# A two-layer token mixer on one core: another load list, layer-1 grouping and TensorE order

## The chip, the core and the metric

The kernel runs on one NeuronCore of a Trainium2 chip. Its engines run side by side, each with its own instruction stream: TensorE (PE in the profile; its weight loads are PEld) multiplies matrices, VectorE (DVE), ScalarE (ACT) and GpSimd (POOL) work on elements, and SyncE (SP) issues most of the DMAs. Streams are ordered among each other only by semaphores. Operands live in SBUF, 128 partitions wide; matmul results go to PSUM, from where ACT and DVE take them. The metric is the device time of one execution in microseconds (us), lower is better.

## What is computed

The input x has 2048 tokens of 512 features in bf16; w1 and w2 are 512×512, w3 is 512×1792 and w4 is 1792×512.

```
h  = gelu(layernorm(x) @ w1)
hs = [quarter 0 of h moved by +1 token, quarter 1 by -1, quarter 2 by +2, quarter 3 by -2] @ w2
x1 = x + hs
out = x1 + gelu(layernorm(x1) @ w3) @ w4
```

Tokens shifted in from outside are zeros. The layer norms have no learned weights.

## The kernel before

**Tiles.** The 2048 tokens are 16 tiles of 128. A tile's layer norm is numbered q: 0 to 15 are the first layer norm, 16 to 31 the second (q = 16 + tile). Everything of x, the weights, the hidden layers and the normalised tiles stays in SBUF.

**One token tile's way.** Its x is loaded (L368). Statistics come either from DVE (bn_stats L416, bn_aggr L418) or, for the q in `STAT_ACT`, from ACT passes that sum (L395, L400) and small DVE steps (L405, L408, L412). POOL raises the variance to the power -0.5 (L423). The normalisation runs on DVE (L445), ACT (L454) or POOL (L457), as `NORM` says for that q; for ACT and POOL a further small step, nmr (L450), runs on DVE or POOL as `NMR` says. The normalised tile is then transposed, either by TensorE into PSUM (L490; `ty:q` in the order) with a copy back by ACT, DVE or half each (`EVAC`, L498), or by a transposing DMA that SP issues (`tp`, L463). Tiles that have a `ty` or `sa` in the order go by TensorE, and a `tp` entry for them in the load list is then skipped.

**Matmuls.** `up1:g` (L626) multiplies a group of tiles by w1; `GROUPS[1]` lists how many tiles each group holds, in tile order. A gelu on ACT (L641) moves the result to hT. `mix:t` (L666) multiplies the shifted h of one tile by w2, so it needs h of the tile and of its two neighbours; DVE adds x and writes x1 (L673, L677), after which the second layer norm of the tile starts. `up2:g` multiplies a group of tiles by w3 in 14 chunks of 128 features, up to 1024 columns of PSUM at a time, each followed by a gelu on ACT. `down:t` (L695) multiplies one tile by w4 in 14 matmuls, DVE adds x1 (L703), and the tile is stored (L706). The last tile goes in three parts of 256, 160 and 96 columns (`TAIL`).

**Tile 0** goes another way, to start early. It is centred only, its x is the stationary operand: `sa:0 sb:0` are the two halves of its transposition, `ra:0 rb:0` the two halves of its product with w1 (L528; part a reads the first half of w1, part b the second), a gelu on ACT with the scale (L569) follows, then `th:0` transposes the result on TensorE (L594) and DVE copies it (L604, `HEV`).

**Warm-up.** `warm:n` is n matmuls on zeros (L720) before the first real work.

**Who orders what.** The order on TensorE is `SCRIPT` (L274), written out. `LOADS` (L271) is the order of the loads: `x4-5` is one DMA of two tiles, `@act` puts a load on ACT's ring instead of SP's, `w1a` and `w1b` are halves of a weight, a bare `w3` is all of it. The loads' priority puts them ahead of everything else on SP. The streams of ACT, DVE, POOL and SP are made by a planner (`order` and `place`): it computes from TensorE's order when each operation is due, starting at `DUE`, adds the wishes of `BIAS`, and plays the program through with written-down durations, taking on each engine the most urgent operation that is ready within a look-ahead (`LOOK`). `LAG` is what it adds to a load's landing. The planner runs on the host, and only the order of the instructions comes from it. On the chip each engine runs its stream strictly in that order.

In PSUM there are three pairs of banks for y (transposed tiles, up1, up2) and two single banks for o (warm-up, th, mix, down), each used in turn.

Of the kernel before, what the change touches and what calls it, by code (L numbers as in the profile page):

```python
# [25 lines left out]
class Program:  # L26
# [2 lines left out]

    HOP = {"pe": 200.0, "dve": 155.0, "act": 220.0, "pool": 120.0, "sp": 70.0}  # L30
    LOOK = {"dve": 300.0, "act": 300.0}
    DUE = 164483.0
    BEGIN = {"sp": 30.0, "act": 150.0, "pe": 400.0, "dve": 150.0, "pool": 450.0}
    ENTRY = 1900.0
    COLD, RESTART = 4300.0, 800.0
    LAG = {"load": 750, "tp": 700}

    def __init__(self):
        self.ops = []
# [12 lines left out]
    def order(self):  # L52
# [58 lines left out]
        assert seen == len(self.ops), "cycle"  # L111
        if self.DUE:

            topo, left = [], [len(d) for d in preds]
            stack = [i for i, n in enumerate(left) if n == 0]
            while stack:
                i = stack.pop()
                topo.append(i)
                for j in succs[i]:
                    left[j] -= 1  # L120
                    if left[j] == 0:
                        stack.append(j)
            due, t = {}, self.DUE
            for op in self.ops:
# [12 lines left out]
        for op in self.ops:  # L137
            op.prio += BIAS.get(op.name, 0.0)
            if op.first is not None:
# [11 lines left out]
    def place(self, succs, order_only):  # L151
# [46 lines left out]
        def land(op):  # L198
            nonlocal moved, last
            if op.queue == "tp":  # L200
                at = max(clock + 500.0, op.start + 2450.0, last + 600.0) + self.LAG["tp"]
            elif op.name.startswith("out"):
                at = clock + 300.0
                self.total = max(self.total, at)
            else:
                moved += op.dur
                at = clock + 600.0 + min(600.0, 0.3 * moved) + (600.0 if op.dur > 1400.0 else 0.0)
                at += self.LAG["load"] if moved > 1200.0 else 50.0
            if op.queue != "tp":
# [47 lines left out]
        self.seq = out  # L257
        return out

GROUPS = {1: (1, 1, 1, 1, 2, 1, 4, 2, 2, 1), 2: (2, 4, 4, 2, 4)}  # L260
NORM = {0: "act", 3: "act", 7: "pool", 8: "act", 9: "pool", 10: "pool", 11: "pool", 12: "pool", 14: "act", 15: "act", 16: "pool", 18: "act", 19: "act", 24: "pool", 25: "act", 26: "pool", 27: "pool", 29: "pool", 30: "pool", 31: "act"}
EVAC = {0: "both", 1: "both", 2: "both", 4: "both", 8: "both", 9: "dve", 10: "dve", 11: "dve", 12: "dve", 13: "dve", 14: "dve", 16: "dve", 17: "dve", 19: "both", 20: "both", 21: "both", 22: "both", 23: "both", 24: "dve", 25: "both", 27: "both", 29: "both", 30: "both", 31: "both"}
STAT_ACT = (0, 7, 9, 12, 13, 15, 18, 21, 25, 29, 30)
TAIL = (256, 160, 96)
NMR = {0: "pool", 1: "pool", 3: "pool", 5: "pool", 6: "pool", 7: "pool", 8: "pool", 9: "pool", 11: "pool", 13: "pool", 14: "pool", 15: "pool", 16: "pool", 17: "pool", 18: "pool", 20: "pool", 21: "pool", 22: "pool", 26: "pool", 27: "pool", 28: "pool", 29: "pool", 31: "pool"}
NAT = (0,)
SPLIT = (0,)
CSPLIT = ()
HEV = {0: "dve", 4: "dve"}
BIAS = {}  # L270
LOADS = """  # L271
x1 x2 tp2 x0@act w1a w1b x3 x4-5 tp5 w2a w2b x6-7 w3 tp17 w4a x8-10 w4b tp6 x11-12 tp1 tp16 x13-15
"""
SCRIPT = """  # L274
warm:9 sa:0 sb:0 ty:1 ra:0 rb:0 ty:2 up1:1 th:0 up1:2 mix:0 ty:3 ty:5 mix:1 ty:4 up1:3-4 ty:16 mix:2 ty:17
mix:3 up2:0 mix:4 up1:5 down:1 down:0 mix:5 up1:6-7 mix:8 mix:6 up1:9 mix:9-10 up1:8 mix:7 mix:11 up2:1
mix:13 mix:15 up2:3 down:5 mix:12 up2:2 mix:14 down:2 down:4 down:3 down:6-8 down:11 down:9 up2:4 down:10
down:12-15
"""

def bass_standalone__mixer_s_mlp__prompt_kernel(nc, x, w1, w2, w3, w4, out):
# [3 lines left out]
    NT, DC, FC = S // P, D // P, F // P  # L285
    groups = {l: [(sum(GROUPS[l][:i]), n) for i, n in enumerate(GROUPS[l])] for l in GROUPS}
    NXN, NO, NPAIR, NOB, NJ = 16, 4, 3, 2, 4
# [8 lines left out]
    with ExitStack() as es:  # L296
# [87 lines left out]
        def ln(layer, t):  # L384
# [3 lines left out]
            col = lambda a: a[:, q : q + 1]  # L388
            how = NORM.get(q, "dve")
            sign = -1.0 if q in NAT and how == "act" else 1.0  # L390
            if q in STAT_ACT:
                if layer == 1:
# [22 lines left out]
            else:  # L415
# [4 lines left out]
                       writes=[(("mv", q), 0), (("vpe", q), 0)], dur=75)  # L420
            var = vpe[:, q : q + 1] if q in STAT_ACT else mv[:, q, 1:2]
            pg.add("pool", f"rstd{q}",
# [3 lines left out]
            if q in NAT:  # L426
                assert how != "act" or q in STAT_ACT

# [18 lines left out]
            else:  # L447
                eng = NMR.get(q, "dve")
                pg.add(eng, f"nmr{q}",
# [17 lines left out]
        def pe_transpose(t, q, pair):  # L467
            layer = 1 if q < NT else 2
            how = EVAC.get(q, "act")
            if pair:  # L470
# [104 lines left out]
        def h_transpose(t):  # L575
            g = group_of[1, t]
            how = HEV.get(t, "act")
            k = NAT.index(t)
# [71 lines left out]
        def mm_mix(t):  # L650
# [20 lines left out]
            wr = [(("x1", t), 0)]  # L671
            if NT + t in STAT_ACT:
                f = lambda e: e.scalar_tensor_tensor(x1_sb[:, t, :], dst, 1.0, x_sb[:, t, :], ALU.mult, ALU.add,  # L673
# [198 lines left out]
```

## Time and profile before

| what | value |
|---|---|
| median of 4 runs | 135.41 us (135.33 to 135.69) |
| the profiled execution's own time | 135.33 us |
| its span, first to last instruction | 134.0 us |
| granted TensorE clock | 1.0 all through |
| POOL, busiest 40th of the span | 0.9 of the slice |
| HBM read, written | 6.82 MB, 2.10 MB |

When the loads went out and landed, in us from the start of the span:

| load | issued | landed after |
|---|---|---|
| x1, x2 (SP) | 0.08, 0.54 | 2.4, 2.6 |
| x0 (ACT) | 0.21 | 2.6 |
| w1a, w1b | 0.99, 1.46 | 4.3, 4.5 |
| x3, x4-5 | 2.07, 2.5 | 4.3, 4.6 |
| w3 (1792 KB) | 4.51 | 9.3 |
| x8-10 | 5.57 (SP held 3.5) | 13.2 |
| w4b | 9.15 (SP held 1.9) | 12.1 |

SP's first transposing DMA (tile 6) was issued at 15.33, then x11-12 and x13-15, then six more transposes from 19.21 on. The second up1 group that needs a transposing DMA started at 30.8.

How to read it: a busy share is an average over the whole span, so it doesn't tell which engine sets the end. The chain of waits does: it goes back from the last instruction, at each step to what released it. A TensorE piece in the chain that follows another TensorE piece without a gap means that TensorE was never waiting there.

### The profile page before, as it was taken

How to read it: one execution, taken by the hardware profiler on the slowest of the kernel's cores; microseconds unless marked ns; L12 is line 12 of the kernel's file. 1: busy time of each engine (PE TensorE's matmuls, PEld its weight loads, DVE VectorE, ACT ScalarE, POOL GpSimd, SP SyncE). 2: the span in 40 equal slices, each digit the busy share in tenths (PEclk: the TensorE clock that was granted, in tenths of full speed). 3: DMA queues.
4: the chain of work that ended last, by engine and by line, in shares of the span. 5: the costliest groups of instructions: out<-in, count | busy, mean ns of one | idle time of the engine just before them, and what ended most of it. 6: DMA issues, size and time to landing. Idle time of an engine off the chain costs nothing.

```text
span 134.0 us, 2001 instructions
## 1 busy us (share of the span) xinstructions
PE 130.9 (98%) x776; PEld 71.7 (53%) x789; DVE 50.2 (37%) x134; ACT 58.4 (44%) x92; POOL 29.8 (22%) x68
## 2 busy tenths in 40 slices
PE   8999999999999999999999999999999999999994
PEld 3487687544666444478444444444444444444464
DVE  2799976756188920070070004232222200012223
ACT  6798359979625375547225553000000155520000
POOL 2444449892103850015010002100000000000000
PEclk9999999999999999999999999999999999999999
DMA  5999998555452134100311000311111100001112
GB/s 156 306 387 395 352 282 235 89 81 110 86 116 84 39 77 82 39 0 18 65 39 39 0 0 0 78 39 44 39 41 66 49 0 0 0 5 39 39 39 78
DMA packets 21290, 12.19 MB, mean 91 GB/s; under 512 B 13857, under 2 KB 20769, under 8 KB 21281
## 3 DMA queue, kind: packets, MB, share of 16 engines
q1 hardware_dynamic: 20704, 11.80, 33.2%
q10 hardware_dynamic: 576, 0.26, 0.7%
q8 instruction: 6, 0.10, 0.3%
q14 instruction: 4, 0.02, 0.1%
HBM read 6.82 MB, written 2.10 MB: 67 GB/s over the span
## 4 chain that ended last, share of the span: by engine, by line
PE 94%; DMA 3%; SPq 1%; issue 1%; DVE 0%
PE y_ps L626 46%; PE o_ps L695 36%; PE o_ps L666 10%; DMA w_sb<-in_w_dram 3%; PE y_ps L490 1%; SPq L368 1%; PE y_ps L528 0%; SPq L377 0%; DVE o_sb L703 0%; PE o_ps L594 0%; SPq L857 0%
## 5 line engine op out<-in xcount | busy, mean ns | idle before, releaser
L626 PE MATMUL y_ps<-xnT,w_sb 128*128 128x512 bf16 (+2 forms) x421 | 63.4, 308 | 0.2
L626 PEld LDWEIGHTS y_ps<-xnT,w_sb 128*128 128x128 bf16 x424 | 38.3, 98 | 24.9
L641 ACT ACTIVATE h2T<-y_ps 128x1024 bf16<-128x1024 f32 (+1 forms) x29 | 28.6, 994 | 48.8 <-PE y_ps L626 48.6
L695 PE MATMUL o_ps<-w_sb,h2T 128*128 128x512 bf16 (+3 forms) x247 | 48.6, 355 | 0.3
L695 PEld LDWEIGHTS o_ps<-w_sb,h2T 128*128 128x128 bf16 x252 | 23.6, 98 | 24.7
L703 DVE TENSOR_TENSOR o_sb<-o_ps,x_sb 128x512 bf16<-128x512 f32 (+3 forms) x18 | 11.4, 631 | 46.9 <-PE o_ps L695 46.9
L423 POOL TENSOR_TENSOR rstd<-mv,neghalf 128x1 f32<-128x1 f32 x21 | 11.5, 549 | 22.9 <-DVE mv L418 14.0
L416 DVE BATCH_NORM_STATS2 st<-x_sb 128x6 f32<-128x512 bf16 x21 | 14.1, 678 | 3.3 <-DMA x_sb<-in_x_dram 3.2
L666 PE MATMUL o_ps<-w_sb,hT 128*128 128x512 bf16 x59 | 14.9, 379 | 0.3
L423 POOL TENSOR_TENSOR rstd<-vpe,neghalf 128x1 f32<-128x1 f32 x11 | 6.0, 548 | 29.4 <-DVE vpe L412 29.3
L673 DVE SCALAR_TENSOR_TENSOR x_sb<-o_ps,x_sb 128x512 bf16<-128x512 f32 x5 | 3.4, 683 | 19.0 <-PE o_ps L666 19.0
L641 ACT ACTIVATE hT<-y_ps 128x512 bf16<-128x512 f32 (+1 forms) x10 | 8.1, 805 | 5.1 <-PE y_ps L626 5.0
L666 PEld LDWEIGHTS o_ps<-w_sb,hT 128*128 128x128 bf16 x64 | 6.0, 98 | 5.7
L677 DVE TENSOR_TENSOR x_sb<-o_ps,x_sb 128x512 bf16<-128x512 f32 x11 | 7.5, 683 | 3.7 <-PE o_ps L666 3.6
L457 POOL TENSOR_SCALAR xn_buf<-x_sb,rstd,nmr 128x512 bf16<-128x512 bf16 x11 | 8.4, 765 | 0.8 <-DVE nmr L450 0.4
L400 ACT ACTIVATE junk<-x_sb 128x512 bf16<-128x512 bf16 x11 | 6.9, 624 | 2.2 <-DVE x_sb L673 2.2
L454 ACT ACTIVATE xn_buf<-x_sb,nmr,rstd 128x512 bf16<-128x512 bf16 x8 | 6.3, 807 | 1.2 <-POOL nmr L450 1.1
L445 DVE TENSOR_SCALAR xn_buf<-x_sb,mv,rstd 128x512 bf16<-128x512 bf16 x12 | 5.3, 443 | 2.8 <-POOL rstd L423 2.6
L720 PE MATMUL o_ps<-zeros 128*128 128x512 bf16 x9 | 4.0, 631 | 0.4 <-DVE zeros L347 0.4
L395 ACT ACTIVATE junk<-x_sb 128x512 bf16<-128x512 bf16 x6 | 3.7, 624 | 0.7 <-DMA x_sb<-in_x_dram 0.7
L418 DVE BATCH_NORM_AGGREGATE mv<-st 128x2 f32<-128x9 f32 x21 | 3.8, 189 | 0.3
L450 POOL TENSOR_SCALAR nmr<-mv,rstd 128x1 f32<-128x1 f32 x13 | 3.4, 263 | 0.7
(34 smaller groups left out, 28.5 us busy)
## 6 DMA issues: line engine op xcount, KB each, us to landing
out_dram<-o_sb SPq DMA_DIRECT2D x15, 128.0 KB, 1.7
w_sb<-in_w_dram SPq DMA_DIRECT2D x1, 1792.0 KB, 9.3
w_sb<-in_w_dram SPq DMA_DIRECT2D x2, 896.0 KB, 11.8
w_sb<-in_w_dram SPq DMA_DIRECT2D x4, 256.0 KB, 4.7
x_sb<-in_x_dram SPq DMA_DIRECT2D x3, 256.0 KB, 5.1
x_sb<-in_x_dram SPq DMA_DIRECT2D x2, 384.0 KB, 9.5
x_sb<-in_x_dram SPq DMA_DIRECT2D x3, 128.0 KB, 2.6
xnT<-xn_buf SPq DMA_TRANSPOSE x24, 2.5
```

The costliest lines, as they stand in the source:

```text
L400: (lambda d: (lambda e: e.activation(d, src, ACT_F.Square, accum_out=sums[:, q, 1:2])))(junk[:, b, :]),
L416: pg.add("dve", f"bnst{q}", lambda e: e.bn_stats(st9[:, q, 0:6], src), reads=rs, writes=[(("st", q), 0)], dur=605)
L423: lambda e: e.tensor_tensor(col(rstd), var, neghalf[:], ALU.pow),
L445: lambda e: e.tensor_scalar(dst, src, mv[:, q, 0:1], rstd[:, q : q + 1], ALU.subtract, ALU.mult),
L454: f = lambda e: e.activation(dst, src, ACT_F.Identity, bias=nmr[:, q : q + 1], scale=rstd[:, q : q + 1])
L457: f = lambda e: e.tensor_scalar(dst, src, rstd[:, q : q + 1], nmr[:, q : q + 1], ALU.mult, ALU.add)
L626: ins = e.matmul(y_ps[:, p, W * i : W * (i + 1)], wsb[:, dc, P * fc : P * (fc + 1)], src[:, dc, P * t0 : P * t0 + W], start=(dc == 0), sto ...
L641: (lambda d, s: (lambda e: e.activation(d, s, ACT_F.Gelu_apprx_tanh)))(dst, ysrc),
L666: ins = e.matmul(dst, hT[:, j, c0 : c0 + P], w2_sb[:, j, :], start=(j == 0), stop=(j == DC - 1))
L677: f = lambda e: e.tensor_tensor(x1_sb[:, t, :], dst, x_sb[:, t, :], ALU.add)
L695: ins = e.matmul(dst, h2T[:, fc, P * t : P * (t + 1)], w4_sb[:, fc, cs], start=(fc == 0), stop=(fc == FC - 1))
L703: (lambda d, c: (lambda e: e.tensor_tensor(o_sb[:, oi, c], d, x1_sb[:, t, c], ALU.add)))(dst, cs),
```

## The change

The load list is rewritten: x0 and x1 come in one load on SP's ring, first of all; x3, x4 and x5 come alone; w3 comes in two halves with x6 between; w4 is one load, after x7-9 and x11; x10, x15 and x12-14 follow it. The `tp` entries all name tiles that TensorE transposes.

Layer 1's groups change from tiles 0, 1, 2, 3, 4-5, 6, 7-10, 11-12, 13-14, 15 to 0, 1, 2, 3, 4, 5, 6-7, 8-9, 10-13, 14-15. The order on TensorE changes: eleven warm-up matmuls instead of nine; `mix:0` and `mix:1` together after `ty:3`; `up1:5` ahead of `up2:0`; other sequences of mix, up2 and down later. The tables that place statistics, normalisation and copies on engines change, `BIAS` is filled, and two constants of the planner change.

```
-    DUE = 164483.0
+    DUE = 30468.4
...
-    LAG = {"load": 750, "tp": 700}
+    LAG = {"load": 450, "tp": 700}
...
-GROUPS = {1: (1, 1, 1, 1, 2, 1, 4, 2, 2, 1), 2: (2, 4, 4, 2, 4)}
+GROUPS = {1: (1, 1, 1, 1, 1, 1, 2, 2, 4, 2), 2: (2, 4, 4, 2, 4)}
-NORM = {0: "act", 3: "act", 7: "pool", 8: "act", 9: "pool", 10: "pool", 11: "pool", 12: "pool", 14: "act", 15: "act", 16: "pool", 18: "act", 19: "act", 24: "pool", 25: "act", 26: "pool", 27: "pool", 29: "pool", 30: "pool", 31: "act"}
+NORM = {0: "act", 4: "act", 5: "act", 6: "pool", 8: "pool", 9: "pool", 10: "act", 11: "act", 12: "act", 13: "pool", 14: "act", 15: "act", 18: "pool", 19: "pool", 20: "pool", 21: "act", 24: "act", 28: "act", 29: "act", 30: "pool", 31: "act"}
-EVAC = {0: "both", 1: "both", 2: "both", 4: "both", 8: "both", ... }
+EVAC = {0: "dve", 2: "both", 4: "both", 5: "dve", 8: "dve", ... }
-STAT_ACT = (0, 7, 9, 12, 13, 15, 18, 21, 25, 29, 30)
+STAT_ACT = (0, 9, 12, 14, 15, 20, 23, 24, 25, 27, 30)
...
-HEV = {0: "dve", 4: "dve"}
-BIAS = {}
+HEV = {0: "dve", 4: "dve", 5: "dve", 6: "dve"}
+BIAS = {"bnag15": 607.808, "bnag16": -502.345, "bnag2": -211.967, ... "nmr7": 1640.92, ... "x1_8": -1394}
 LOADS = """
-x1 x2 tp2 x0@act w1a w1b x3 x4-5 tp5 w2a w2b x6-7 w3 tp17 w4a x8-10 w4b tp6 x11-12 tp1 tp16 x13-15
+tp4 x0-1 x2 w1a w1b tp17 x3 x4 x5 w2a w2b tp5 tp3 tp5 w3a x6 w3b x7-9 x11 tp1 w4 tp0 x10 x15 x12-14
 """
 SCRIPT = """
-warm:9 sa:0 sb:0 ty:1 ra:0 rb:0 ty:2 up1:1 th:0 up1:2 mix:0 ty:3 ty:5 mix:1 ty:4 up1:3-4 ty:16 mix:2 ty:17
-mix:3 up2:0 mix:4 up1:5 down:1 down:0 mix:5 up1:6-7 mix:8 mix:6 up1:9 mix:9-10 up1:8 mix:7 mix:11 up2:1
-mix:13 mix:15 up2:3 down:5 mix:12 up2:2 mix:14 down:2 down:4 down:3 down:6-8 down:11 down:9 up2:4 down:10
-down:12-15
+warm:11 sa:0 sb:0 ty:1 ra:0 rb:0 ty:2 up1:1 th:0 up1:2 ty:3 mix:0-1 ty:4 up1:3-4 ty:5 mix:2 ty:16 mix:3
+ty:17 up1:5 up2:0 mix:4 down:1 up1:6 down:0 up1:7 mix:6 mix:5 up1:8 mix:8 mix:7 up1:9 mix:9 mix:11 up2:1
+mix:10 mix:14 up2:2 mix:13 mix:12 up2:3 mix:15 down:5 down:4 down:3 down:9 down:2 down:6 down:10 down:7
+down:11 up2:4 down:8 down:13 down:12 down:14-15
 """
```

In the `EVAC` and `BIAS` lines the dots stand for entries left out; `NMR` changes in the same manner and is not shown. `NAT`, `SPLIT` and `TAIL` stay.

More of the change, by code (lines that the diff above doesn't have):

```diff
@@ L258, in place @@
         return out
-GROUPS = {1: (1, 1, 1, 1, 2, 1, 4, 2, 2, 1), 2: (2, 4, 4, 2, 4)}
-NORM = {0: "act", 3: "act", 7: "pool", 8: "act", 9: "pool", 10: "pool", 11: "pool", 12: "pool", 14: "act", 15: "act", 16: "pool", 18: "act", 19: "act", 24: "pool", 25: "act", 26: "pool", 27: "pool", 29: "pool", 30: "pool", 31: "act"}
-EVAC = {0: "both", 1: "both", 2: "both", 4: "both", 8: "both", 9: "dve", 10: "dve", 11: "dve", 12: "dve", 13: "dve", 14: "dve", 16: "dve", 17: "dve", 19: "both", 20: "both", 21: "both", 22: "both", 23: "both", 24: "dve", 25: "both", 27: "both", 29: "both", 30: "both", 31: "both"}
-STAT_ACT = (0, 7, 9, 12, 13, 15, 18, 21, 25, 29, 30)
+GROUPS = {1: (1, 1, 1, 1, 1, 1, 2, 2, 4, 2), 2: (2, 4, 4, 2, 4)}
+NORM = {0: "act", 4: "act", 5: "act", 6: "pool", 8: "pool", 9: "pool", 10: "act", 11: "act", 12: "act", 13: "pool", 14: "act", 15: "act", 18: "pool", 19: "pool", 20: "pool", 21: "act", 24: "act", 28: "act", 29: "act", 30: "pool", 31: "act"}
+EVAC = {0: "dve", 2: "both", 4: "both", 5: "dve", 8: "dve", 10: "both", 11: "dve", 13: "dve", 14: "both", 15: "both", 16: "both", 17: "dve", 20: "dve", 22: "dve", 23: "both", 25: "both", 26: "both", 29: "dve", 30: "dve", 31: "both"}
+STAT_ACT = (0, 9, 12, 14, 15, 20, 23, 24, 25, 27, 30)
 TAIL = (256, 160, 96)
-NMR = {0: "pool", 1: "pool", 3: "pool", 5: "pool", 6: "pool", 7: "pool", 8: "pool", 9: "pool", 11: "pool", 13: "pool", 14: "pool", 15: "pool", 16: "pool", 17: "pool", 18: "pool", 20: "pool", 21: "pool", 22: "pool", 26: "pool", 27: "pool", 28: "pool", 29: "pool", 31: "pool"}
+NMR = {0: "pool", 2: "pool", 3: "pool", 7: "pool", 9: "pool", 12: "pool", 13: "pool", 17: "pool", 18: "pool", 21: "pool", 22: "pool", 23: "pool", 25: "pool", 26: "pool", 27: "pool", 28: "pool", 30: "pool", 31: "pool"}
 NAT = (0,)
@@ L268 @@
 CSPLIT = ()
-HEV = {0: "dve", 4: "dve"}
-BIAS = {}
+HEV = {0: "dve", 4: "dve", 5: "dve", 6: "dve"}
+BIAS = {"bnag15": 607.808, "bnag16": -502.345, "bnag2": -211.967, "bnag23": -1845, "bnag4": -1313.82, "bnst19": 1481.28, "bnst8": 1255.94, "mean10": -299, "mean13": 763, "msq0": -855.016, "msq10": 1022, "nmr14": -806.788, "nmr7": 1640.92, "ssq0": -262.973, "ssq2": 507, "ssq24": -171, "sum15": -1347, "sum19": 698.515, "tp28": 663, "vpe0": -383, "vpe13": -986, "vpe18": 383, "x1_11": 1071, "x1_13": 325, "x1_2": -117, "x1_8": -1394}
 LOADS = """
-x1 x2 tp2 x0@act w1a w1b x3 x4-5 tp5 w2a w2b x6-7 w3 tp17 w4a x8-10 w4b tp6 x11-12 tp1 tp16 x13-15
+tp4 x0-1 x2 w1a w1b tp17 x3 x4 x5 w2a w2b tp5 tp3 tp5 w3a x6 w3b x7-9 x11 tp1 w4 tp0 x10 x15 x12-14
 """
 SCRIPT = """
-warm:9 sa:0 sb:0 ty:1 ra:0 rb:0 ty:2 up1:1 th:0 up1:2 mix:0 ty:3 ty:5 mix:1 ty:4 up1:3-4 ty:16 mix:2 ty:17
-mix:3 up2:0 mix:4 up1:5 down:1 down:0 mix:5 up1:6-7 mix:8 mix:6 up1:9 mix:9-10 up1:8 mix:7 mix:11 up2:1
-mix:13 mix:15 up2:3 down:5 mix:12 up2:2 mix:14 down:2 down:4 down:3 down:6-8 down:11 down:9 up2:4 down:10
-down:12-15
+warm:11 sa:0 sb:0 ty:1 ra:0 rb:0 ty:2 up1:1 th:0 up1:2 ty:3 mix:0-1 ty:4 up1:3-4 ty:5 mix:2 ty:16 mix:3
+ty:17 up1:5 up2:0 mix:4 down:1 up1:6 down:0 up1:7 mix:6 mix:5 up1:8 mix:8 mix:7 up1:9 mix:9 mix:11 up2:1
+mix:10 mix:14 up2:2 mix:13 mix:12 up2:3 mix:15 down:5 down:4 down:3 down:9 down:2 down:6 down:10 down:7
+down:11 up2:4 down:8 down:13 down:12 down:14-15
 """
```

## The prediction

> **What bounds the kernel now.** I read the page first, for the busy shares, then the chain of waits in order of time, then the timeline of the first 12 us by engine, and last the moved bytes in short stretches.
>
> ```profile
> PE 130.9 (98%) x776; PEld 71.7 (53%) x789; DVE 50.2 (37%) x134; ACT 58.4 (44%) x92; POOL 29.8 (22%) x68
> ```
>
> TensorE is at 98% while no other engine reaches half. A busy share proves little by itself, so the chain must say whether TensorE is late or merely filled:
>
> ```profile
> 1.42 0.04 issue
> 1.47 4.51 DMA w_sb<-in_w_dram
> 5.98 0.05 issue
> 6.02 0.61 PE y_ps L528 x2
> ...
> 22.37 0.81 PE o_ps L666 x3
> 23.18 0.89 PE y_ps L626 x16
> 24.07 6.04 PE o_ps L695 x28
> ...
> 132.24 0.26 DVE o_sb L703
> ```
>
> The columns are start, length, what. One load (the second half of w1) is waited for until 5.98; from 6.02 (the second half of token tile 0's rows, rb:0 in the order) to 132.24 all pieces are TensorE's. To see that there is no slack in these 126.22 us I add up the work by the pieces' own lengths. up1 of one tile 0.89, of two 1.75, of four 3.45: five, three and one give 13.15. Sixteen mixes at 0.865 are 13.84. up2 is 6.11 twice and 12.1 three times: 48.5. Fifteen downs at 3.03 and the last in three parts (128.68 to 132.24, less the end of the one before, 3.1) are 48.6. Six transposed tiles and th:0 at 0.225 are 1.6, rb:0 0.43. Sum 126.1. So at most about 0.1 us is stall (the visible one is ty:4, which started at 10.99 instead of about 10.87). Two terms only can move the end: when rb:0 starts, and stalls behind it.
>
> **What the change leaves alone.** The new group list of layer 1 holds the same sizes in another sequence (without tile 0: five of one, three of two, one of four), and the same tiles go through TensorE (0 to 5, 16, 17). So the 126.1 us of work are equal, and the tail (256, 160, 96) too. A gain can only be an earlier start, 0.1 us apart. DUE shifts all due times alike and orders nothing anew.
>
> **The start, step by step.**
>
> ```profile
> 0.44 4.02 PE L720 MATMUL o_ps<-zeros 128*128 128x512 bf16 x9 [0.44 <-DVE zeros L347]
> ...
> 4.19 0.90 PEld L490 LDWEIGHTS y_ps<-ident,xn_buf 128*128 128x128 bf16 x8 [0.64 <-POOL rstd L423]
> ...
> 4.71 0.38 ACT L498 ACTIVATE xnT<-y_ps 128x256 bf16<-128x256 bf16 x1 [0.24 <-PE y_ps L490]
> 4.97 0.29 DVE L498 COPY xnT<-y_ps 128x256 bf16<-128x256 bf16 x1 [0.27 <-PE y_ps L490]
> ...
> 5.34 0.11 PEld L528 LDWEIGHTS y_ps<-w_sb,xnT 128*128 128x128 bf16 x2 [0.25 <-DMA w_sb<-in_w_dram]
> ...
> 6.02 0.11 PEld L528 LDWEIGHTS y_ps<-w_sb,xnT 128*128 128x128 bf16 x2 [0.57 <-DMA w_sb<-in_w_dram]
> ```
>
> Before, three things end well ahead of w1: the nine warm-up matmuls at 4.26, tile 0's transposes from there, its copies on ACT and DVE at 5.08 and 5.26. Rows part a waits for w1a (5.34), part b for w1b (6.02).
>
> *Loads.* x0 leaves ACT's ring and shares a load with x1. Ahead of w1b stand the same 393 KB of x and 262 KB of w1a; SP still issues three loads before it, one of them with twice the rows (estimate 0.45 instead of 0.39 us, from w1a's 0.43 for as many rows): w1b goes out 0.05 later. Before, x1 landed at 2.5 and x0 at 2.8; together I put both at 2.75, so ACT's sums of x0 start as before, and tile 1's statistics lose 0.25, under cover of the warm-up. A landing of w1b at 5.7 to 6.3 is possible; its row says 5.98, and I keep 6.03.
>
> *Warm-up.* Two more matmuls on zeros. Their starts are 0.427 us apart, and weight loads after them still last 0.15 us up to the one at 4.94, against 0.098 later: the clock was slow until about 5.1. So eleven end at 0.44+11×0.427 = 5.14. Here the Trainium skill speaks otherwise: "TensorE: Matmul & The Clock Gate", Part 1, has the warm-up as some 3.4 us of activity, not a number of matmuls, with full speed after it. By that the clock rises near 3.85, warm-ups nine to eleven cost 0.216 each (half of 0.427), all end at about 4.5, and w1b stays the bound: shift 0.05. By the row the shift is what follows. I take the row, since it is this very start.
>
> *Copies.* Tile 0's first copy began 0.45 after its first transpose with the slow clock; with the fast one 0.06+0.22+0.03 = 0.31. From 5.14 that is 5.45 to 5.59. Both copies now run on DVE, 0.28 each in turn, instead of on ACT and DVE side by side: the first ends at 5.73 to 5.87, rows part a starts 0.07 later, takes 0.43, and part b follows at **6.23 to 6.37** instead of 6.02; the second copy (by 6.15) is hidden behind part a. The landing of w1b is now hidden, and only past 6.2 is it late. If a normalisation (0.41) stands before the copy on DVE, up to 0.4 more; if the clock rises sooner, 0. I take **+0.25**, ends 0 and +0.6.
>
> **7 to 16 us.** The order is now ty:3 mix:0-1 ty:4 up1:3-4 ty:5 mix:2 ty:16 mix:3 ty:17 up1:5. Norm 3 goes from ACT (0.81) to DVE (0.41), norm 4 and 5 from DVE to ACT. DVE and ACT are 0.8 to 1.0 busy here, so this is where order bites. At about 8.1 DVE has both h's copy (0.42) and norm 3 (0.41) to do, ty:3 and mix:0 wait for one each, at 8.9 and 9.1: 0 to 0.2 late. ACT needs norm 4 (0.81) and gelu of up1:2 (0.59) between 8.5 and 9.9, for mix:1 and ty:4: they just fit if norm 4 is first, else ty:4 is 0.3 late. Behind norm 4 on ACT stands the copy of tile 3 (0.59) for up1:3 at 11.1. Against that stands the 0.12 at ty:4 that could go. Ends −0.12 and +0.6; I take **+0.1**. The x loads split into single tiles move no bytes: the windows from 8 to 13 us carry 384 to 412 GB/s with loads of every size. So they cost 0.
>
> **The move of up1:5 and down:1.** up1:5 used to stand between mix:4 and down:1:
>
> ```profile
> 21.48 1.51 ACT L641 ACTIVATE h2T<-y_ps 128x1024 bf16<-128x1024 f32 x2
> ...
> 22.37 0.81 PE L666 MATMUL o_ps<-w_sb,hT 128*128 128x512 bf16 x3
> ```
>
> The two gelus end at 22.99 (up2:0 ended at 22.14). down:1 reads all of them; before, mix:4 and up1:5 covered until 23.91. Now only mix:4 does: TensorE is free at 22.14+0.87 = 23.01, the gelus end at 22.99, and from ACT's end to the weight load was 0.11 after gelu of tile 0 (7.42 to 7.53), then 0.05 to the matmul. So down:1 starts at 23.15: **+0.13** (0 to +0.7, if ACT has a sum of 0.63 in front).
>
> **w4 and SP's queue.** down:1 is due 0.9 earlier and reads all of w4. The bytes up to w4's end are the same 6.16 MB before and after, as x4 to x9 and x11 stand before it; w4b landed at 21.25 (issued 9.15, 12.1 us), so 1.8 us are left. What follows in the queue:
>
> ```profile
> 18.00:19.00 1.00, 1.00 (x12) 0.89 (x10) 0.20 (x1) 1.00 (x2) 0.84 (x2) 1.00 1.12 336
> 19.00:20.00 1.00, 1.00 (x12) 0.90 (x10) 1.00 (x2) 0.89 (x4) 0.18 (x1) 1.00 2.87 170
> 20.00:21.00 1.00, 1.00 (x12) 0.90 (x10) 0.78 (x7) 1.00 (x2) 0.73 (x2) 1.00 0.07 22
> 21.00:22.00 1.00, 1.00 (x12) 0.90 (x10) 0.21 (x1) 0.89 (x3) 1.00 (x3) 1.00 1.03 292
> ```
>
> The last number is GB/s. At 20 to 21 the DMA engines stand nearly still, around the first transposing DMA (issued 15.33, landed 21.7). All tp entries of the new load list name tiles that TensorE turns, so they fall away, and every load is issued before any transposing DMA: that hole goes, the x loads end about 1 us sooner. SP was held 3.5 us at the issue of x8-10; behind the 1792 KB of w4 it will be held again, for x10, x15, x12-14, and the transposes of tiles 6 and 7 wait behind them. Loads end at some (6.82−6.16)/0.355 = 1.9 us after w4's last byte (19.4), so 21.3; then tile 6 lands at about 22.8 and tile 7 at 24.1 (1.3 us each, the transposes' spacing). up1:6 needs tile 7 at 26.2, where the old order needed its second group of transposes at 30.8. Hidden, with 2 us left: 0. The skill's "DMA: Bandwidth & Descriptors" (Rules for kernel authors) tells to coalesce, and its Anatomy section gives about 2 us of fixed cost for each load (issued by GpSimd there): were that paid in turn, two loads more than before would bring tile 7 to 28.1 and cost 1.9. The windows from 8 to 13 us, 384 to 412 GB/s through loads of every size, show no such pause, so I stay at 0. w3 in two lands about 0.3 sooner (131 KB less before its end), due at 16: 0.
>
> **Sum.** 0.25+0.1+0.13 = +0.48 on the profiled execution, whose own time is 135.33 with a span of 134.0. That makes 135.81; the median shown is 0.08 above that execution, so **135.9**.
>
> **Rivals.** A measurement here tells a change from none at about 0.2%, 0.27 us.
> - *Nothing to see.* The start is held by w1b after all (+0.05), the hole at down:1 is 0.13 and ty:4's 0.12 goes: +0.06, 135.5. For it: before, an order made by the same planner ran dense. Against: the slow weight load at 4.94. Chance 0.20.
> - *Faster.* If the slow clock ends at 4.3, warm-up ends at 4.7, part a can start at 5.34 and part b at 5.77; with x0 off the second ring, w1b must land by 5.7. Then −0.25, and ty:4's 0.12 on top: 135.0. It decides from w1b before 5.75. For it: at 2.5 to 4.5 us the engines moved just 150 to 250 GB/s, so w1 could come sooner. Against: both conditions must hold. Chance 0.13.
> - *A wait that takes the place.* Tile 7's transpose, in SP's queue behind the held loads, lands after 26.2; each slot lost is 1.3 us, so two or three too many give +0.6 to +1.9; or ACT runs gelu, copies and norm 4 in the wrong sequence at 9 to 11, and each wrong turn is 0.6 to 0.8. With the start's 0.25: about 136.7. For it: both engines full, 18 loads against 16. Against: 2 us of slack. Chance 0.20.
> - The forecast, +0.27 to +0.8 (135.7 to 136.2): 0.47.
>
> Slower 0.47+0.20 = 0.67, same 0.20, faster 0.13. The range 135.2 to 136.8 leaves out most of the faster case and the worst of the late transposes, together about 0.2.
>
> **What would show it.** Right: eleven warm-ups ending near 5.1; part a waiting for DVE's copy, not for a load; part b at about 6.25; a gap of 0.1 to 0.2 before the first down with ACT's gelu as releaser; no gap before up1:6. Wrong: part b at 6.02 or earlier; a wait of TensorE above 0.4 anywhere later; a sum of TensorE's pieces other than 126.1.

## The result and the profile after

The changed kernel takes 135.77 us (median of 43 runs, 135.31 to 137.03), the one before, timed beside it, 135.58 (64 runs, 135.04 to 136.37). The medians lie 0.19 apart; the ratio of the runs timed side by side is 1.0024 with a 95% interval of 1.0013 to 1.0034, that is some 0.33 us slower, and "no change" lies outside the interval. The profiled execution took 135.99, with a span of 134.7; that is an execution in the upper half, 0.66 above the one profiled before.

First the line of busy shares, then the chain of waits in order of time (start, length, what):

```profile
PE 131.5 (98%) x779; PEld 71.9 (53%) x791; DVE 51.2 (38%) x142; ACT 60.6 (45%) x93; POOL 26.5 (20%) x60
```

```profile
9.60 0.22 DVE nmr L450
9.82 0.04 issue
9.86 1.67 PE o_ps L666 x7
...
15.94 7.01 PE y_ps L626 x72
22.95 0.05 issue
23.00 0.81 PE o_ps L666 x3
23.81 3.09 PE o_ps L695 x14
26.91 1.75 PE y_ps L626 x16
...
132.90 0.26 DVE o_sb L703
```

TensorE is again the bound, and again all but without gaps from part b on. Two places need a second reading. At 9.86 the chain leaves TensorE, for nmr on DVE and from there back to the landing of x3 at 6.99. But mix:0 and mix:1 are eight matmuls, and the chain has seven from 9.86 on. The weight loads of TensorE show where the eighth was:

```profile
9.37 0.27 PEld L490 LDWEIGHTS y_ps<-ident,xn_buf 128*128 128x128 bf16 x4
9.59 1.45 PEld L666 LDWEIGHTS o_ps<-w_sb,hT 128*128 128x128 bf16 x8
```

mix:0's first load follows those of ty:3 at once, so the record of one matmul of 0.22 is missing, and there was no wait. The other place is down:1: up1:5 and up2:0 run in one piece, mix:4 follows, then down:1 takes 3.09 instead of 3.02, a wait of 0.07. The profile names nmr on DVE as its releaser (ended at 23.65). The true one is the second of these two gelus, which end at 23.63:

```profile
22.11 1.51 ACT L641 ACTIVATE h2T<-y_ps 128x1024 bf16<-128x1024 f32 x2 [0.72 <-PE y_ps L626]
```

down:1's first weight load follows at 23.70, and in all nine profiles with this order on TensorE it follows the gelu's end by 0.07, whatever releaser is named. up1:6 follows down:1 at once at 26.9; tile 7's transpose had landed at 25.0 (issued 20.8, 4.2 us). Now the timeline of the start:

```profile
5.09 0.72 PE L490 MATMUL y_ps<-ident,xn_buf 128*128 128x128 bf16 x8
5.52 0.29 DVE L498 COPY xnT<-y_ps 128x256 bf16<-128x256 bf16 x1 [0.43 <-PE y_ps L490]
5.84 0.28 DVE L498 COPY xnT<-y_ps 128x256 bf16<-128x256 bf16 x1
5.96 0.11 PEld L528 LDWEIGHTS y_ps<-w_sb,xnT 128*128 128x128 bf16 x2 [0.32 <-DMA w_sb<-in_w_dram]
6.72 0.11 PEld L528 LDWEIGHTS y_ps<-w_sb,xnT 128*128 128x128 bf16 x2 [0.64 <-DMA w_sb<-in_w_dram]
```

The transposes start at 5.09 instead of 4.26, and DVE makes both copies, one after the other. But the bracketed releasers of the last two lines say that rows part a and part b both waited for w1, which landed at 5.9 and 6.7 here. From part b to the last step of the kernel it is 132.90−6.72 = 126.18 us, as against 126.22 before: the 0.09 at ty:4 is gone, and the 0.07 at down:1 has come. So the whole difference of these two executions is the start of part b, 6.72 for 6.02, and in this profile a load sets it, not the chain of warm-up and copies that I had reckoned with. One execution can't tell whether that is the change or the scatter of a landing. That is what the runs had to decide.

### The profile page after: what moved, and what is told of

Its sections match the earlier page's. It is cut to its first block, busy times and chain, and to the rows that moved or that the text cites. A ratio compares the mean times of both kernels' runs of the same rounds, so it can differ in the third digit from the quotient of the medians.

```text
span 134.7 us, 2009 instructions
## 1 busy us (share of the span) xinstructions
PE 131.5 (98%) x779; PEld 71.9 (53%) x791; DVE 51.2 (38%) x142; ACT 60.6 (45%) x93; POOL 26.5 (20%) x60
## 4 chain that ended last, share of the span: by engine, by line
PE 91%; DMA 4%; DVE 2%; issue 1%; POOL 0%; DVEq 0%
PE y_ps L626 44%; PE o_ps L695 36%; PE o_ps L666 10%; DMA x_sb<-in_x_dram 4%; DVE st L416 1%; PE y_ps L490 1%; POOL rstd L423 0%; DVE mv L418 0%; DVE o_sb L703 0%; DVE nmr L450 0%; DVE xnT L498 0%; DVEq L821 0%
## 5 line engine op out<-in xcount | busy, mean ns | idle before, releaser
L677 DVE TENSOR_TENSOR x_sb<-o_ps,x_sb 128x512 bf16<-128x512 f32 x10 | 6.8, 681 | 22.9 <-PE o_ps L666 22.9
L454 ACT ACTIVATE xn_buf<-x_sb,nmr,rstd 128x512 bf16<-128x512 bf16 x12 | 9.6, 806 | 2.8 <-POOL nmr L450 2.8
L400 ACT ACTIVATE junk<-x_sb 128x512 bf16<-128x512 bf16 x11 | 6.8, 619 | 2.8 <-DVE x_sb L673 2.7
L457 POOL TENSOR_SCALAR xn_buf<-x_sb,rstd,nmr 128x512 bf16<-128x512 bf16 x8 | 6.1, 763 | 1.0 <-DVE nmr L450 0.8
L720 PE MATMUL o_ps<-zeros 128*128 128x512 bf16 x11 | 4.9, 632 | 0.4 <-DVE zeros L347 0.4
L673 DVE SCALAR_TENSOR_TENSOR x_sb<-o_ps,x_sb 128x512 bf16<-128x512 f32 x6 | 4.1, 680 | 1.3 <-PE o_ps L666 1.3
L450 DVE TENSOR_SCALAR nmr<-mv,rstd 128x1 f32<-128x1 f32 x12 | 2.5, 206 | 3.9 <-POOL rstd L423 3.8
L395 ACT ACTIVATE junk<-x_sb 128x512 bf16<-128x512 bf16 x5 | 3.1, 623 | 1.9 <-DMA x_sb<-in_x_dram 1.9
## 6 DMA issues: line engine op xcount, KB each, us to landing
w_sb<-in_w_dram SPq DMA_DIRECT2D x1, 1792.0 KB, 14.6
```

Of the source, the lines that this page charges most:

```text
L400: (lambda d: (lambda e: e.activation(d, src, ACT_F.Square, accum_out=sums[:, q, 1:2])))(junk[:, b, :]),
L454: f = lambda e: e.activation(dst, src, ACT_F.Identity, bias=nmr[:, q : q + 1], scale=rstd[:, q : q + 1])
L457: f = lambda e: e.tensor_scalar(dst, src, rstd[:, q : q + 1], nmr[:, q : q + 1], ALU.mult, ALU.add)
L677: f = lambda e: e.tensor_tensor(x1_sb[:, t, :], dst, x_sb[:, t, :], ALU.add)
```

## The experiments

**Theory A** is the prediction's: TensorE's own chain (eleven warm-ups, transposes, copy, part a) keeps part b from starting before 6.2 to 6.4. **Theory B**, which the profile after suggests, is that the new head of the load list brings w1 later. Every variant was timed in five rounds beside the kernel before; the interval of its ratio, in brackets, is about as wide as the effect itself, so that most single variants can't decide.

### Undo one part, or do one part alone

Nine warm-ups in the changed kernel; only the number of matmuls is cut, so that no other stream changes:

```
-                for _ in range(n):
+                for _ in range(n - 2):
```

> The changed kernel with nine warm-up matmuls instead of eleven, every other stream the same. Theory A (the start is held by TensorE's own chain: eleven warm-ups, then both copies of tile 0 on DVE): transposes from 4.6 instead of 5.1 (normalisation of tile 0 ready by then), rows part b 0.3 to 0.4 us sooner, time 0.2 to 0.4 us less than the changed kernel, ratio to before 1.000 to 1.001. Theory B (the second half of w1 lands later because of the new head of the load list): part b still waits for w1b, time unchanged, ratio 1.002 to 1.003, and w1b lands at 6.5 or later in the profile.

Measured: 135.43 us, ratio 0.9997 (0.9970 to 1.0024). The excess is gone from the median with the load list untouched; the interval just reaches the changed kernel's ratio. The profiled execution shows something else besides: transposes from 4.24 and a first copy at 4.85, as Theory A has it, but then part a and part b at the slow clock (1.48 us for the four matmuls, 1.02 in the next variant), so that part b still started at 6.15 only:

```profile
5.29 1.48 PE L528 MATMUL y_ps<-w_sb,xnT 128*128 128x512 bf16 x4
```

The old head of the load list in the changed kernel:

```
-tp4 x0-1 x2 w1a
+tp4 x1 x2 x0@act w1a
```

> The changed kernel with the old head of the load list (x1 and x2 on SP's ring, x0 on ACT's), other streams the same. Theory A: unchanged, ratio 1.002 to 1.003, part b bound by the copy on DVE at about 6.3. Theory B: w1b lands at about 6.0 again, part b starts at about 6.3 instead of 6.7, ratio about 1.001 or less.

Measured: 135.82, ratio 1.0021 (1.0001 to 1.0040). The excess stays, and here the copy holds the start as Theory A has it: part a and part b run in one piece behind it (part b at 6.01+0.43 = 6.44, w1b landed at 6.4):

```profile
5.57 0.29 DVE L498 COPY xnT<-y_ps 128x256 bf16<-128x256 bf16 x1 [1.08 <-PE y_ps L490]
6.01 1.02 PE L528 MATMUL y_ps<-w_sb,xnT 128*128 128x512 bf16 x4
```

The new head alone in the kernel before:

```
-x1 x2 tp2 x0@act w1a
+x0-1 x2 tp2 w1a
```

> The kernel before with the new head of the load list alone (x0 and x1 in one load on SP's ring, then x2). Theory A: no change, 0.999 to 1.001, since w1b lands as before at about 6.0. Theory B: w1b lands 0.3 to 0.7 us later and all of it shows, ratio 1.002 to 1.005.

Measured: 135.59, ratio 1.0001 (0.9980 to 1.0023). Nothing to see within that interval; w1b landed at 6.3.

Eleven warm-ups alone in the kernel before (`range(n + 2)`):

> The kernel before with eleven warm-up matmuls, other streams the same. Theory A: transposes from 5.1, the slower copy ends at 5.8 to 5.9, part b starts at 6.3 to 6.4 instead of 6.0, ratio 1.002 to 1.003. Theory B (where w1b often lands late): 0 to 0.1 us, ratio 1.000 to 1.001.

Measured: 135.83, ratio 1.0012 (0.9989 to 1.0034), by the ratio undecided. Its profile is not: w1b had landed at 5.7, and part a started at 6.05, released by ACT's copy, with no load in sight (timeline, TensorE):

```profile
6.05 1.02 PE L528 MATMUL y_ps<-w_sb,xnT 128*128 128x512 bf16 x4 [0.23 <-ACT xnT L498]
```

Parts a and b run in one piece there, so part b starts at 6.05+0.43 = 6.48. By themselves these four can't tell the number of warm-ups from the head of the list: both variants with nine have the new head, both with eleven the old one. If the head did matter, the new one would be the faster, the reverse of Theory B. The two kernels themselves fill the table: the kernel before has nine and the old head (135.45 beside these four), the changed one eleven and the new head (135.77). The six medians line up with the warm-ups (nine: 135.43, 135.45, 135.59; eleven: 135.77, 135.82, 135.83). So Theory B falls as the main cause, though a small part of it isn't excluded, and it doesn't fall as a fact about single executions: with one and the same load list w1b landed at 6.7 in the changed kernel and at 5.6 in the variant with nine warm-ups.

### The terms of the start by themselves

The two copies of tile 0 side by side again, in the changed kernel:

```
-EVAC = {0: "dve"
+EVAC = {0: "both"
```

> The changed kernel with tile 0's two copies side by side on ACT and DVE, as before the change (the planner's streams differ in a few places, mostly after 20 us). Theory A as predicted (only the first copy is on the path, the second is hidden behind rows part a): no gain, ratio 1.002 to 1.003, since ACT's copy lasts 0.38 and DVE's 0.29. Rival A2 (it is the two copies in turn on DVE that cost the start): 0.2 to 0.3 us less than the changed kernel, ratio about 1.000.

Measured: 135.90, ratio 1.0026 (1.0006 to 1.0047). No gain, as reckoned: rival A2's 1.000 lies outside the interval. Its profile adds nothing on this, as w1 (5.8 and 6.5) held both parts in that execution.

Fifteen warm-ups in the changed kernel (`range(n + 4)`):

> The changed kernel with fifteen warm-up matmuls, other streams the same. Theory A: the clock is fast from 5.1 to 5.4, so three of the four further ones last 0.216 each and rows part b starts at about 7.1 instead of 6.3 to 6.7: ratio to before 1.007 to 1.009. If the slow clock goes on as long as the warm-up does (0.427 each): 1.012 to 1.015. Theory B (landing of w1b alone holds the start): 1.002 to 1.003 until part b is at 6.7.

Measured: 136.46, ratio 1.0060 (1.0042 to 1.0078): more warm-up costs time, some 0.5 us for four by the ratios and 0.7 by the medians. Its profile shows little of this at the start, because in that execution the clock rose early: up to 3.4 the weight loads stand 0.43 apart, from 3.84 on six of them fit into 1.2 us, and part b starts at 6.54, sooner than in the profiled execution of the changed kernel. What this execution lost is a wait at mix:0 (weight loads of TensorE):

```profile
10.10 0.99 PEld L666 LDWEIGHTS o_ps<-w_sb,hT 128*128 128x128 bf16 x6 [0.66 <-DVE nmr L450]
```

The named releaser is not the true one. That nmr ended at 9.6, and mix:0 doesn't read it. mix:0 does read w2, whose second half was issued at 4.01 and took 5.9 us to land: 9.88. In five of the profiles mix:0 came after a wait (0.1 to 0.7 us), and in all five its first weight load follows the landing of w2b by 0.21 to 0.22, so w2b is what it waited for.

Seven warm-ups in the changed kernel (`range(n - 4)`):

> The changed kernel with seven warm-up matmuls, other streams the same. Theory A: the warm-up ends at 3.4 and is no longer in the way; tile 0's transposes start with its normalisation at 4.2 to 4.7, part b with w1b. If the clock needs the two matmuls more, rows and first up1 run slow (0.43 instead of 0.22 us per two transposes or matmul of 512 columns) for up to 1 us: ratio 1.001 to 1.006. If not: 0.999 to 1.001, like nine.

Measured: 136.67, ratio 1.0063 (1.0034 to 1.0093). The times fall into two groups, three at 135.3 to 135.6 and eight at 136.3 to 137.1. The profiled execution is of the first group, with fast weight loads from the first transposes on (two in 0.13 us):

```profile
4.27 0.13 PEld L490 LDWEIGHTS y_ps<-ident,xn_buf 128*128 128x128 bf16 x2 [1.57 <-issue]
4.61 0.11 PEld L490 LDWEIGHTS y_ps<-ident,xn_buf 128*128 128x128 bf16 x2 [0.21 <-ACT xn_buf L431]
```

Before these TensorE stood idle for 0.7 us. That the second group is executions in which the clock did not rise in time is the likely reading, but no profile shows one of them; the nearest is the execution with nine above, whose clock rose at 6.2. Nine warm-ups end at about the time at which tile 0's normalisation is ready, and of the changed kernel's twelve runs with nine only two lie above 136.2.

### Take w1 off the path

The second half of w1 on ACT's ring, in the kernel before:

```
-x0@act w1a w1b x3
+x0@act w1a w1b@act x3
```

> The kernel before with the second half of w1 issued on ACT's ring, at about 0.6 us instead of 1.46. If the landing of w1b is held by its place in SP's ring: w1b lands 0.2 to 0.5 us sooner, part b starts at 5.7 to 5.8, ratio 0.997 to 0.999. If it is held by the bytes that the sixteen engines share: x1, x2 and w1a land later by what w1b lands sooner, w1a becomes the bound, ratio 1.000 to 1.003.

Measured: 135.40, ratio 0.9989 (0.9972 to 1.0007). w1b landed at 4.1, but w1a at 5.7 became the bound, and part b started at 6.17. So the order within w1 was the wrong one, and the first half went to ACT's ring instead:

```
-x0@act w1a w1b x3
+x0@act w1a@act w1b x3
```

> The kernel before with the first half of w1 on ACT's ring (issued at about 0.6 us), the second on SP's (at about 1.0 instead of 1.46); other streams the same. If a second ring moves w1 sooner, as one execution with w1b on it suggests: w1a lands at about 4.1, w1b at 5.3 to 5.7, TensorE's own chain (nine warm-ups) becomes the bound, part b starts at 5.75 to 5.8, 0.2 to 0.4 us sooner: ratio 0.997 to 0.9985. If the bytes alone decide: w1b at about 6.0, ratio 0.9995 to 1.001.

Measured: **135.15, ratio 0.9965 (0.9947 to 0.9983)**, faster than both kernels. w1a landed at 4.3 and w1b at 5.1; part a starts at 5.23, right behind the transposes, with no load to wait for, and part b at 5.66.

With both bounds of the start in hand, the theories part clearly. The changed kernel with x0 and w1a on ACT's ring, first with nine, then with its eleven warm-ups:

```
-tp4 x0-1 x2 w1a w1b
+tp4 x1 x2 x0@act w1a@act w1b
...
-                for _ in range(n):
+                for _ in range(n - 2):
```

> The changed kernel with nine warm-ups and the first half of w1 and x0 on ACT's ring. Theory A: both bounds of the start are gone, part b at 5.75 to 5.8, ratio 0.997 to 0.999. If the changed order on TensorE or its streams cost something of their own behind the start: 1.000 to 1.002.

Measured: 135.20, ratio 0.9975 (0.9959 to 0.9990). With the same warm-ups and the same head of the list, the changed kernel and the kernel before are 0.05 apart (135.20 and 135.15): the order on TensorE, the groups, the tables and the later loads cost or bring nothing that shows.

> The same with the eleven warm-ups of the changed kernel. Theory A: w1 lands before 5.8, yet part b cannot start before 6.2 to 6.4 (warm-up until 5.1, copy on DVE, part a), ratio 1.001 to 1.002, 0.3 to 0.5 us above the nine. Theory B (only w1's landing counts): as with nine warm-ups, 0.997 to 0.999.

Measured: 135.67, ratio 1.0003 (0.9985 to 1.0021), 0.47 above the nine; between these two kernels nothing differs but the number of warm-ups. The timelines of the two, nine first (DVE's copies, TensorE's rows):

```profile
4.72 0.29 DVE L498 COPY xnT<-y_ps 128x256 bf16<-128x256 bf16 x1
5.16 1.02 PE L528 MATMUL y_ps<-w_sb,xnT 128*128 128x512 bf16 x4
```

```profile
5.46 0.29 DVE L498 COPY xnT<-y_ps 128x256 bf16<-128x256 bf16 x1 [0.62 <-PE y_ps L490]
5.90 1.02 PE L528 MATMUL y_ps<-w_sb,xnT 128*128 128x512 bf16 x4
```

w1 had landed by 5.3 in both. Two warm-ups more move the first copy by 0.74 and the rows by as much: part b at 6.33 instead of 5.59. With w1 out of the way, Theory A is shown. Of the twelve runs with eleven, three were at 134.8 to 135.1, as low as with nine; executions in which the clock rises early would do that, but none of them was profiled.

### The second load on the edge

Two profiles had mix:0 wait long for w2 (old head 0.3, fifteen warm-ups 0.7; with seven warm-ups it was 0.2, with nine and w1a on ACT's ring 0.1). So, in the changed kernel, x5 behind w2:

```
-x3 x4 x5 w2a w2b tp5 tp3 tp5 w3a
+x3 x4 w2a w2b x5 w3a
```

> The changed kernel with x5 loaded behind w2 instead of ahead of it; compute streams the same. If w2's second half, due at mix:0 at about 9.6, is at times the last to come (two executions of other variants had mix:0 wait 0.3 and 0.7 for it): it lands 0.3 to 0.5 sooner, the runs at 136.5 and above become rare, ratio 1.001 to 1.002. If not: unchanged, 1.002 to 1.003, with some runs at 136.5 and above.

Measured: 135.46, ratio 1.0007 (0.9991 to 1.0022), no run above 136.2. By the times that is as the guess had it, by the profile it isn't: w2b was issued 0.5 sooner and yet landed at 9.5 (3.5 plus 6.0), not sooner than in the changed kernel (9.2), and mix:0 waited 0.4 for it at 9.7. The scatter of a landing is as large as the effect; the interval holds both readings. Seven of the 43 runs of the changed kernel lie at 136.5 to 137.0. What these are stays open: the variants with the old head, with w1a on ACT's ring and with w2 first had none in 48 runs, the one with nine warm-ups had one in twelve, the one with the copies side by side two in twelve, and no such run was profiled. The profile with w2 first also shows eleven warm-ups over by 4.6, with weight loads of 0.10 instead of 0.15 us at 4.19: the clock rose at about 4.1 there.

### All starts side by side

Every time in us from the start of the span, one execution each; "rest" is from part b to the last step.

| kernel | w1b landed | part b | rest |
|---|---|---|---|
| before | 6.0 | 6.02 | 126.22 |
| changed | 6.7 | 6.72 | 126.18 |
| changed, nine warm-ups | 5.6 | 6.15 | 126.20 |
| changed, old head | 6.4 | 6.44 | 126.46 |
| before, new head | 6.3 | 6.29 | 126.22 |
| before, eleven warm-ups | 5.7 | 6.48 | 126.37 |
| changed, copies side by side | 6.5 | 6.58 | 126.30 |
| changed, fifteen | 6.1 | 6.54 | 126.84 |
| changed, seven | 5.9 | 5.91 | 126.36 |
| changed, w2 first | 6.4 | 6.41 | 126.64 |
| before, w1b on ACT | 4.1 (w1a 5.7) | 6.17 | 126.21 |
| before, w1a on ACT | 5.1 | 5.66 | 126.37 |
| changed, nine, w1a on ACT | 5.1 | 5.59 | 126.27 |
| changed, eleven, w1a on ACT | 5.3 | 6.33 | 126.18 |

The rest differs by 0.2 at most but for three rows (126.46, 126.64, 126.84), in which mix:0 waited 0.3 to 0.7 for w2b. Part b starts at the later of two times (of the halves of w1, the later counts). One is the landing of w1b, scattered over 5.6 to 6.7 while w1 goes through SP's ring. The other is TensorE's own chain: 5.6 to 5.7 with nine warm-ups, but 6.15 in the execution whose clock stayed slow until then; 6.3 to 6.5 with eleven, but 5.97 at most in the one whose clock rose at about 4.1 (part a at 5.54). Two more warm-ups shift the chain by 0.7, and where w1b is late the chain is hidden behind it; so the mean loss, 0.33, can be less than the shift. How often each of the two comes last is not known from one execution of each kernel: with w1 on SP's ring and eleven warm-ups it was w1 in three profiles of five.

## Why the prediction was right, and where its sizes were off

- **The bound.** That TensorE's work is equal and dense, so that only the start and new stalls count, held: 126.18 for 126.22.
- **The start, +0.25.** The mechanism was right: the number of warm-ups sets TensorE's chain, in both kernels, and the chain came out as worked: first copy 5.45 to 5.59 (measured 5.52), part b at 6.23 to 6.37 (6.33 where w1 was out of the way). Two things were too simple. w1b was taken as one number, 5.98 to 6.03; it scatters over 5.6 to 6.7, so that the term is a mean of the later of two times. And the old start was not well ahead of w1: DVE's copy ended at 5.26 and w1a landed at 5.30, nearly at once; only part b had room, 5.77 for 5.98. Of its own signs, "part a waiting for DVE's copy" and "part b at about 6.25" fail in the profiled execution, where w1 held both parts and part b came at 6.72; they hold in the variants with the old head (6.44) and with w1a on ACT's ring (6.33). That a term worked out between two fixed times comes near the mean of scattered ones is in part luck.
- **Rule against row.** I took the row (slow clock until 5.1) over the Trainium skill's warm-up of some 3.4 us ("TensorE: Matmul & The Clock Gate", Part 1). The trace bears the row out. Its record of the granted clock begins with full speed at 5.04 in the kernel before and at 5.31 in the changed one; of what was granted before that there is no record, so the "1.0 all through" of the table of the kernel before, and the 1.00 of every window before 5 us, say nothing about the start. Five more profiles have such a record, at 4.63 to 5.54. In the others the weight loads and matmuls show it: at about 3.4 to 4.1 in four, near the rule's 3.85, and at 6.2 in the one with nine warm-ups. The first warm-up started at 0.42 to 0.45 in all of them, so the clock rose some 3.0 to 5.8 us after it. No fixed time and no fixed number of warm-ups would have foretold it. The row was one draw from the middle of a wide range, and that it fitted the changed kernel's profile is luck too.
- **7 to 16 us, +0.1.** Off: in the profile after DVE had norm 3 first (8.72), the copy of h second (9.00), and neither ty:3 nor mix:0 was late by them. The term is 0. In its place stands one that the prediction doesn't have: w2b, at 8.5 in the kernel before, landed at 8.1 to 9.9 with the changed order and held mix:0 by 0.1 to 0.7 in five of its eight variants, though not in the profile of the changed kernel itself.
- **down:1, +0.13.** Measured 0.07. ACT was ready when the gelu came.
- **w4 and SP's queue, 0.** Right as a term, too hopeful in its parts. SP was held 6.9 us at the issue behind w4; w4 landed at 22.2 (7.57 plus 14.6), a microsecond later than I put it, still 1.6 before down:1. The last x tiles landed at 24.0, not at 21.3, and no sooner than before (23.8). Tile 7 landed at 25.0 instead of 24.1, 1.9 before up1:6; the 28.1 that a pause for each further load would have made did not come.
- **The sum.** +0.48 was forecast, 135.9; measured +0.33, 135.77. The rival "nothing to see" would have fitted with the warm-ups left at nine. The faster rival named the right place, w1b before 5.75 with the chain at 5.77, and w1a on ACT's ring reached it by another way.

The load list and the new orders, the heart of the change by its words, cost or bring nothing that these runs can show; the two warm-up matmuls make the difference.

## What to carry to other kernels

A kernel whose bound engine is full from its first real instruction to the end can only gain at that first instruction: list everything that it waits for, each with its spread over executions, and treat the start as the latest of them. Filler that keeps an engine warm stands in the same queue as the work; it should end when the first operand comes: here seven pieces cost as much as fifteen (1.0063 and 1.0060), and nine were best of the four numbers tried. A releaser that a profile names is a guess; a delay that is the same in every execution (0.07 behind the gelu, 0.21 behind w2b) tells more. When a wait changes its releaser from one execution to the next, undo one suspect at a time with all streams held equal before the profile of a single execution is believed.

## What the runs showed that was not expected

Taking half of w1 to the second ring may have done more than save the issue time. Moved bytes in windows of half a microsecond, the kernel before and then the same with w1a on ACT's ring (the last two numbers are the DMA share and GB/s):

```profile
3.00:3.50 0.50, 0.50 (x3) 0.23 (x2) 0.47 (x3) 0.50 (x2) 0.00 (x0) 1.00 1.05 147
3.50:4.00 0.50, 0.50 (x3) 0.06 (x1) 0.49 (x1) 0.47 (x3) 0.49 (x1) 1.00 0.81 186
```

```profile
3.00:3.50 0.50, 0.50 (x3) 0.22 (x2) 0.43 (x2) 0.50 (x2) 0.00 (x0) 1.00 1.10 389
3.50:4.00 0.50, 0.50 (x3) 0.04 (x1) 0.43 (x1) 0.47 (x2) 0.45 (x1) 1.00 1.04 363
```

The dip after the first x tiles, 147 to 186 GB/s, is gone (363 to 389), and w1b lands 0.9 us sooner for an issue that is 0.5 sooner. All four kernels with half of w1 on ACT's ring ran at 272 to 389 GB/s in these two windows, the ten others at 84 to 311. But the dip is not a matter of the ring alone: two of those ten hardly had it, with all of w1 on SP's ring (the old head at 282 and 294, eleven warm-ups in the kernel before at 311 and 266). From issue to landing w1b took 4.1 to 4.3 us in the three with w1a on ACT's ring and 4.1 to 5.1 in the ten. So a second ring may spare the dip, which is not shown, and why the dip comes and goes was not found out.
